# Releasing loads and indirect sends by a count of TensorE instructions, in a local attention and mixture-of-experts kernel

## The chip, the cores and the metric

The kernel runs on 1 core of one Trainium2 chip. The metric is device time in microseconds (us) of one execution, as a median of several runs. Engines are named as in the profile: PE is TensorE's matmul part and PEld its weight loads, DVE is VectorE, ACT ScalarE, POOL GpSimd, SP SyncE. "SPq" and "POOLq" are the sequencers of these engines, which issue DMAs.

## The reference, cut to what matters

Attention comes first: 8 batches, 8 heads, 512 local and 32 global tokens, head size 64. A local query sees the 32 global keys and the local keys within 32 places; a global query sees all. Then each of the 4,608 token rows (512 wide) goes to the one expert of eight that its cosine logit chooses, through two matrices with a ReLU between them.

```python
s_ll = scale * np.matmul(q_l, k_l.transpose(0, 1, 3, 2))
mask = np.abs(pos[:, None] - pos[None, :]) <= window            # window = 32
...
out_l = np.matmul(sm(concat[s_lg, s_ll]), concat[v_g, v_l])
out_g = np.matmul(sm(s_g), v_all)
...
expert_idx = argmax(xn @ en.T / tau)
h = np.maximum(x[mask] @ w1[e], 0.0)
out[mask] = gate_w[mask, None] * (h @ w2[e])
```

## The kernel before, in words

**Two stages.** The first, up to about 238 us, does attention and routing; the second, from about 290 us to the end, runs the experts item by item (`item`, 128 rows at a time, 2 MB of weights for each). Between them lie the last batch's routing, a first block of the expert work in plain f32, and the wait for the table of items.

**Steps of the first stage.** A step `g` is a quarter of a batch (32 steps, and two more to drain). `slot(g)` writes out one step by hand, phase after phase, with automatic reordering off: `scores(g)`, sends, the transposes `turned(g-1)`, `maxima`, `exps`, then `values(g-2)`, and the routing of the batch before (`turn`, `logits`, `back`, `place`, `placed`) with the global tokens' work (`g_scores`, `g_turned`, `g_values`) where `plan` puts it. So three steps are in the air at once, and ACT and DVE have a step's time between the matmuls that feed them and those that need them.

**Instructions of a step.** A f32 matmul is two weight loads and two matmuls on the PE queue, 4 instructions in all; a transpose or a bf16 matmul is 2. One batch (four steps) is scores 448, transposes `turned` 64, `values` 512, `g_values` 192, `g_scores` 64, `g_turned` 24, routing 82: 1,386 instructions, 346 a step.

**Loads.** `loads[g]` lists the DMAs of step `g`, all issued by SP in program order: four of `load_v` (values, tile `vt`, six buffers) and, in most steps, two of `load` (queries and keys, tile `raw`, two buffers); late steps add `fetch_w` (expert weights, tile `stg`), and steps 4 to 7 one `first_fill` each. `deal` takes a step's list at the step's start. `tick(ins, part)` stands at six places of a step (halves of `scores`, end of `turned`, two in `values`, end of `turn`): it sets `state["mark"]` to the PE instruction just written and issues the next sixth of the list. `paced` makes each of these DMAs wait for the mark.

```python
def tick(ins, part):
    state["mark"] = ins
    while parts and share[0] * 6 < part * share[1]:
        parts.pop(0)()
        share[0] += 1
```

**Sends.** When a batch is routed, POOL scatters its rows to their expert's place in HBM with indirect DMAs (`send`, L794, 128 rows each). For batches 0 to 4 these are 20 sends, one a step, in phase SEND behind `scores`, each waiting for the last matmul of that step's scores. POOL also copies the global tokens' rows (L637) and runs a memset for each batch's `choose`.

Of the kernel before, what the change touches and what calls it, by code (L numbers as in the profile page):

```python
# [12 lines left out]
F32 = mybir.dt.float32  # L13
# [17 lines left out]
NE = 8  # L31
# [29 lines left out]
MW = 5 * P  # L61

GCUT = 3


def _window(i):
# [34 lines left out]
def tile_kernel(ctx: ExitStack, tc: tile.TileContext, qk, va, emb, tau, wraw, cst, out):  # L101
# [41 lines left out]
    def give(x, g2, ob):  # L143
# [9 lines left out]
            oob_is_err=False,  # L153
        )

    def early_block(x, h, hT, ob, acc, acc2):


        def turn(src, acc=acc):
            o = acc()  # L160
            for c in range(4):
                nc.tensor.transpose(o[:, c * P : (c + 1) * P], src[:, c * P : (c + 1) * P], ident)
            return o

        st = {}

        def begin(xT, acc):
            st["xT"] = xT
            nc.scalar.copy(xT[:, :512], turn(x, acc))

        def up(nh, ks):
            if ks[0] == 0:
                st["g", nh] = acc()
                if nh == 0:
                    st["h"], st["hT"] = h(), hT()
            for k in ks:
                c = k * 1024 + nh * 512
                nc.tensor.matmul(
                    st["g", nh], st["xT"][:, k * P : (k + 1) * P], cols(st0[0], c, c + 512), start=(k == 0), stop=(k == 3)
                )  # L180
            if ks[-1] == 3:
                nc.scalar.activation(st["h"][:, nh * 512 : (nh + 1) * 512], st["g", nh], AF.Relu)

        def half(nh):
            nc.scalar.copy(st["hT"][:, nh * 512 : (nh + 1) * 512], turn(st["h"][:, nh * 512 : (nh + 1) * 512]))

        def down(ks):
            if ks[0] == 0:
                st["g2"] = acc2()
            for k in ks:  # L190
                nc.tensor.matmul(
                    st["g2"],
                    st["hT"][:, k * P : (k + 1) * P],
                    cols(st0[1], k * 512, (k + 1) * 512),
                    start=(k == 0),
                    stop=(k == 7),
                )
            if ks[-1] == 7:
                give(x, st["g2"], ob())

        return (
            begin,
            lambda: up(0, (0, 1)),
            lambda: up(0, (2, 3)),
            lambda: up(1, (0, 1)),
            lambda: half(0),
            lambda: up(1, (2, 3)),
            lambda: down((0, 1)),
            lambda: half(1),
            lambda: down((2, 3)),  # L210
            lambda: down((4, 5)),
            lambda: down((6, 7)),
        )
# [11 lines left out]
    with ExitStack() as actx:  # L225
# [38 lines left out]
            return after(ins, state["mark"]) if "mark" in state else ins  # L264

        parts = []
        share = [0, 0]

        def tick(ins, part):

            state["mark"] = ins
            while parts and share[0] * 6 < part * share[1]:
                parts.pop(0)()
                share[0] += 1

        def deal(extra):

            while parts:
                parts.pop(0)()
            parts.extend(extra)  # L280
            share[:] = [0, len(parts)]

        def load(b, j, k):

# [67 lines left out]

        def keep_warm(n):
            for _ in range(n):
                nc.tensor.matmul(warm[:, 0], ones[:, :P], ones, start=True, stop=True)  # L355

        zero = pers.tile([P, 1], F32, name="zero")
        nc.gpsimd.memset(zero, 0.0)
# [58 lines left out]
        def setup_turn():  # L417

            em = state["em"]
            ep = bank()  # L420
            for c in range(4):
                nc.tensor.transpose(ep[:, c * NE : (c + 1) * NE], em[:, c * P : (c + 1) * P], ident[:NE, :NE])
            e3 = ep[:, : 4 * NE].rearrange("p (c e) -> p c e", c=4)
            nc.vector.tensor_copy(en[:, :, :NE], e3)

# [15 lines left out]
        def scores(g):  # L441

            b, s = divmod(g, 4)
            raw = state["raw", b]
            state["s", g] = ps = ps_s.tile([P, 2, 512], F32, name="s_ps")
            for k in range(4):
                i = 4 * s + k
                c0 = QW + BQ * _run(_window(i))
                if k // 2 == twin(s):
                    if k % 2 == 0:  # L450
                        for c in range(2):
                            for j in (2 * c, 2 * c + 1):
                                for grp in range(2):
                                    hs = half[grp]
                                    at = 64 * (j % 2)
                                    ins = nc.tensor.matmul(  # L456
                                        ps[at : at + 64, grp, (k + c) * P : (k + c + 1) * P],
                                        raw[hs, j, i * BQ : (i + 2) * BQ],
                                        raw[hs, j, c0 : c0 + P],
                                        start=True,  # L460
                                        stop=True,
                                    )
                else:
                    for j in range(4):
                        for grp in range(2):
                            hs = half[grp]
                            ins = nc.tensor.matmul(  # L467
                                ps[32 * j : 32 * j + 32, grp, k * P : (k + 1) * P],
                                raw[hs, j, i * BQ : (i + 1) * BQ],
                                raw[hs, j, c0 : c0 + P],  # L470
                                start=True,
                                stop=True,
                            )
                if k % 2:
                    tick(ins, 1 + k // 2)
            state["scored"] = ins
            state["nm", g] = sm.tile([P, 8], F32, name="nm")
            state["pb", g] = [sp.tile([P, 512], F32, name="pb") for _ in range(2)]
# [30 lines left out]
        def turned(g, grp):  # L509

            state["tp", g, grp] = pt = bank()
            pb = state["pb", g][grp]
            for k in range(4):
                ins = nc.tensor.transpose(pt[:, k * P : (k + 1) * P], pb[:, k * P : (k + 1) * P], ident)  # L514
            if grp:
                tick(ins, 3)

        def take(g, grp):

# [9 lines left out]
        def values(g):  # L529
# [3 lines left out]
            for grp in range(2):  # L533
                pT = state["pT", g, grp]
                for j in range(4):
                    for k in range(4):
                        ins = nc.tensor.matmul(  # L537
                            po[32 * k : 32 * k + 32, grp, j * VH : (j + 1) * VH],
                            pT[:, col(s, k, j) : col(s, k, j) + 32],
                            vals(b, _window(4 * s + k), grp, j),  # L540
                            start=True,
                            stop=True,
                        )
                tick(ins, 4 + grp)
            state["valued"] = ins

        def normed(g):
# [10 lines left out]
        def g_scores(b, part):  # L558
# [6 lines left out]
            for j in range(4):  # L565
                for grp in range(2):
# [4 lines left out]
                        o = o.rearrange("p (w n) -> p w n", n=96)  # L571
                    else:
                        k = k[:, GCUT * P :]
                    nc.tensor.matmul(o, q, k, start=True, stop=True)  # L574
            gm = state["gm", b]
            for grp in range(2):
                nc.vector.tensor_tensor_reduce(
# [16 lines left out]
        def g_turned(b, part):  # L594
# [2 lines left out]
            state["gt", b, part] = o = bank()  # L597
            if part < 2:
                for c in range(4):
                    nc.tensor.transpose(o[:96, c * P : (c + 1) * P], gp[part][:, c * 96 : (c + 1) * 96], ident)  # L600
            else:
                for c in range(2):
                    for grp in range(2):
                        lo = 416 + 32 * c
                        nc.tensor.transpose(o[:, (2 * c + grp) * P : (2 * c + grp + 1) * P], gp[grp][:, lo : lo + P], ident)

        def g_take(b, part):

# [7 lines left out]
        def g_values(b, grp):  # L616

            og = bank()
            for c, (w, kn) in enumerate(((0, 96), (3, 96), (6, 96), (9, 96), (12, P), (13, P))):
                for j in range(4):  # L620
                    rows = slice(32 * j, 32 * j + 32)
                    nc.tensor.matmul(  # L622
                        og[rows, :VH],
                        gT[:kn, grp, c, rows],
                        vals(b, w, grp, j)[:kn],
# [14 lines left out]
        def route(get, groups, closes=False):  # L640
# [4 lines left out]
            def turn(t):  # L645
# [5 lines left out]
                    st["ss"] = sm.tile([P, NR], F32, name="ss")  # L651
                st["xps", t] = xps = bank()
                for c in range(4):
                    ins = nc.tensor.transpose(xps[:, c * P : (c + 1) * P], x[:, c * P : (c + 1) * P], ident)  # L654

                if t < 4:
                    tick(ins, 6)

            def turn_take(t):

# [13 lines left out]
            def logits(t):  # L674
# [3 lines left out]
                    st["us"] = rt.tile([P, NR * P], F32, name="us", bufs=1)  # L678
                st["u", t] = u = bank()
                for c in range(4):  # L680
                    nc.tensor.matmul(u[32 * c : 32 * c + 32, :n], en[:, c, :], st["xT", t][:, c, :n], start=True, stop=True)  # L681

            def logits_take(t):

# [9 lines left out]
            def back(lo, hi):  # L694
# [2 lines left out]
                    st["lg"] = sm.tile([P, NR, NE], F32, name="lg", bufs=2)  # L697
                st["ut", lo] = ut = bank()
                for t in range(lo, hi):
                    nc.tensor.transpose(ut[:, (t - lo) * P : (t - lo + 1) * P], st["us"][:, t * P : (t + 1) * P], ident)  # L700

            def back_sum(lo, hi):

# [48 lines left out]
            def place():  # L752
# [1 line left out]
                st["pc"] = pc = bank()  # L754

                def add(w, t, lo, hi, start, stop):
                    nc.tensor.matmul(
                        pc[:, lo * NE : hi * NE],
                        w,
                        ohb[:, t : t + hi - lo, :].rearrange("p t e -> p (t e)"),  # L760
# [78 lines left out]
        )  # L839

        plan = {}

        def at(g, phase, f, *args):
            plan.setdefault((g, phase), []).append(lambda: f(*args))
# [28 lines left out]
        for b in range(NB - 1):  # L873
# [17 lines left out]
            for t in range(4):  # L891
# [2 lines left out]
                elif b == NB - 3:  # L894
                    at(g0 + 6 + t // 2, LATE if t % 2 else SEND, r.send, t, "valued" if t % 2 else "scored")
                else:
                    at(g0 + 6 + t, SEND, r.send, t, "scored")

        for b in range(3, NB - 1, 4):
            r, g0 = R["g", b // 4], 4 * b + 7  # L900
# [48 lines left out]
        for g in loads:  # L949
            n = len(loads[g])  # L950
            h = (n + 1) // 2
            loads[g] = [f for pair in zip(loads[g][:h], loads[g][h:] + [None]) for f in pair if f]

        def slot(g):

            def do(phase):
                for f in plan.pop((g, phase), ()):
# [44 lines left out]
        with tc.manual_schedule():  # L1002
            keep_warm(16)
            for g in range(NSTEP + 2):
                slot(g)
            deal([])
            assert not plan, plan


# [382 lines left out]
```

## Time and the profile before

| | us |
|---|---|
| median of 3 runs | 727.18 (725.92 to 728.4) |
| the profiled execution | 725.47 |
| its span in the trace | 723.6 |
| outside the span (725.47 - 723.6) | 1.9 |

The rows below come from the one profiled execution. "issue" as a releaser is time in which an engine waited for nothing that the profile shows. Queue q8 of kind "instruction" carries blocks of the program itself to the engines' sequencers. A row with "xN" stands for N instructions merged.

### The profile page before, as it was taken

Reading aid. Unit: us, or ns where it says so; the run is one execution under the profiler, and the core shown is the slowest. Engines: PE = TensorE matmul, PEld = TensorE weight load, DVE = VectorE, ACT = ScalarE, POOL = GpSimd, SP = SyncE. Lnnn points to the kernel's source line nnn. Section 1 sums busy time; section 2 is a strip of 40 time slices with the busy share of each in tenths; the row PEclk is TensorE's granted clock in tenths of the full one; section 3 lists DMA queues with packets and bytes.
Section 4 is the critical chain, followed back from the end, with each engine's and each line's share of the span. In section 5 each row is a group of like instructions: output and inputs, shape, how many; then the busy total and the mean of one; then the engine's idle time right before and its main releaser. Section 6 shows DMA issues by size and latency. Waiting matters only on the chain.

```text
span 723.6 us, 23361 instructions
## 1 busy us (share of the span) xinstructions
PE 674.1 (93%) x7867; PEld 535.3 (74%) x7869; DVE 422.2 (58%) x1449; ACT 458.6 (63%) x956; POOL 273.0 (38%) x318
## 2 busy tenths in 40 slices
PE   9888878878878998999999999999999999999996
PEld 4666666656756546888888888888888888888885
DVE  2778777888677763545554554545455545455443
ACT  4776767747767365656565666666666656565664
POOL 2011222222212344545454545444454545454543
PEclk9999999999899999999999999999999999999999
DMA  8988989878997257746565665656565746575654
GB/s 274 351 249 258 256 236 279 285 213 292 283 301 227 77 214 267 260 165 249 186 232 205 209 225 193 244 185 248 169 249 179 259 157 240 185 231 206 223 210 156
DMA packets 66588, 165.13 MB, mean 228 GB/s; under 512 B 6548, under 2 KB 14868, under 8 KB 66464
## 3 DMA queue, kind: packets, MB, share of 16 engines
q1 hardware_dynamic: 60704, 145.67, 60.5%
q0 software_dynamic: 5760, 17.87, 7.0%
q8 instruction: 71, 1.16, 0.7%
q14 instruction: 53, 0.43, 0.2%
HBM read 142.49 MB, written 22.07 MB: 227 GB/s over the span
## 4 chain that ended last, share of the span: by engine, by line
PE 88%; issue 5%; DMA 2%; DVE 2%; SPq 1%; ACT 1%; POOL 0%; DVEq 0%; POOLq 0%
PE g L1198 18%; PE g L1199 18%; PE g L1203 18%; PE po L537 5%; PE hps L1221 4%; PE pt L514 4%; PE s_ps L467 4%; PE pt L654 2%; PE xps L1174 2%; PE pt L622 2%; DMA raw<-in_qk_dram 2%; PE po L355 2%; PE pt L574 1%; PE pt L681 1%; PE s_ps L456 1%
## 5 line engine op out<-in xcount | busy, mean ns | idle before, releaser
L1194 DVE TENSOR_TENSOR WL<-stg,WH 128x512 f32 (+1 forms) x144 | 150.5, 1045 | 130.2 <-ACT WH L1192 130.2
L1194 POOL TENSOR_TENSOR WL<-stg,WH 128x512 f32 (+1 forms) x144 | 174.3, 1210 | 88.9 <-ACT WH L1192 87.9
L1192 ACT CAST WH<-stg 128x512 f32 (+1 forms) x288 | 177.4, 618 | 9.2 <-DMA stg<-in_wraw_dram 4.6
L1198 PE MATMUL g<-WH,hH 128*128 (+1 forms) x288 | 119.5, 415 | 0.0
L1198 PE MATMUL g<-WH,xH 128*128 (+1 forms) x288 | 116.0, 403 | 0.0
L1199 PE MATMUL g<-WL,hH 128*128 (+1 forms) x288 | 113.3, 393 | 0.0
L1203 PE MATMUL g<-WH,xL 128*128 (+1 forms) x288 | 112.6, 391 | 0.0
L1199 PE MATMUL g<-WL,xH 128*128 (+1 forms) x288 | 112.5, 390 | 0.0
L147 POOL DMA_INDIRECT out_dram<-ob x37 | 37.2, 1006 | 151.7 <-ACT ob L145 142.4
L507 ACT ACTIVATE pb<-pb,nm 128x128 f32<-128x128 f32 x256 | 80.1, 396 | 11.7 <-DVE nm L490 11.5
L1203 PE MATMUL g<-WH,hL 128*128 (+1 forms) x288 | 83.4, 391 | 0.0
L1224 DVE TENSOR_TENSOR hL<-hps,hH 128x512 fp32r<-128x512 f32 x72 | 49.8, 692 | 53.8 <-ACT hH L1223 53.6
L1203 PEld LDWEIGHTS g<-WH,hL 128*128 128x128 f32 x288 | 54.1, 188 | 12.1
L1203 PEld LDWEIGHTS g<-WH,xL 128*128 128x128 f32 x288 | 54.1, 188 | 11.6
L145 ACT ACTIVATE ob<-g,xr 128x512 f32<-128x512 f32 x36 | 24.8, 688 | 59.5 <-PE g L1203 59.5
L1199 PEld LDWEIGHTS g<-WL,xH 128*128 128x128 f32 x288 | 54.2, 188 | 10.2 <-DVE ob L146 0.2
L1198 PEld LDWEIGHTS g<-WH,xH 128*128 128x128 f32 x288 | 54.2, 188 | 10.2 <-issue 0.2
L1198 PEld LDWEIGHTS g<-WH,hH 128*128 128x128 f32 x288 | 54.4, 189 | 9.5
L1199 PEld LDWEIGHTS g<-WL,hH 128*128 128x128 f32 x288 | 54.4, 189 | 9.1
L1215 ACT ACTIVATE h<-g 128x512 f32<-128x512 f32 x72 | 42.9, 595 | 28.8 <-PE g L1203 28.8
L794 POOL DMA_INDIRECT xs<-xt,si x32 | 32.1, 1004 | 75.9 <-PE pt L514 27.5
L1223 ACT CAST hH<-hps 128x512 fp32r<-128x512 f32 x72 | 42.0, 584 | 24.6 <-PE hps L1221 24.6
(200 smaller groups left out, 985.4 us busy)
## 6 DMA issues: line engine op xcount, KB each, us to landing
stg<-in_wraw_dram SPq DMA_DIRECT2D x36, 2048.0 KB, 9.8
vt<-in_va_dram SPq DMA_DIRECT2D x96, 260.0 KB, 4.7
raw<-in_qk_dram SPq DMA_DIRECT2D x56, 304.0 KB, 5.1
xr<-xs SPq DMA_DIRECT2D x38, 257.0 KB, 2.7
vt<-in_va_dram SPq DMA_DIRECT2D x32, 130.0 KB, 5.1
stg<-in_wraw_dram SPq DMA_DIRECT2D x16, 256.0 KB, 5.5
xs<-fill SPq DMA_DIRECT2D x12, 257.0 KB, 3.0
stg<-in_wraw_dram SPq DMA_DIRECT2D x4, 512.0 KB, 7.1
```

What stands on the lines that cost most here:

```text
L147: nc.gpsimd.indirect_dma_start(out=out[:, :], out_offset=bass.IndirectOffsetOnAxis(ap=ob[:, DM : DM + 1].bitcast(U32), axis=0), in_=ob[:, ...
L507: nc.scalar.activation(pb[:, cs], pb[:, cs], AF.Exp, bias=nm[:, n : n + 1], scale=-1.0)
L537: ins = nc.tensor.matmul(po[32 * k : 32 * k + 32, grp, j * VH : (j + 1) * VH], pT[:, col(s, k, j) : col(s, k, j) + 32], vals(b, _window(4 ...
L794: ins = nc.gpsimd.indirect_dma_start(out=xs[:, :], out_offset=bass.IndirectOffsetOnAxis(ap=st["si"][:, t : t + 1], axis=0), in_=get(t), in ...
L1192: made.append(nc.scalar.copy(WH[:, ds(ra, 1), cs], s3))
L1194: made.append(eng.tensor_tensor(WL[:, ds(r, 1), cs], s3, WH[:, ds(r, 1), cs], ALU.subtract))
L1198: reads.append(nc.tensor.matmul(o.unsqueeze(1), a, WH2[:, ds(rp, 1), sl], start=first, stop=False))
L1199: reads.append(nc.tensor.matmul(o.unsqueeze(1), a, WL2[:, ds(rp, 1), sl], start=False, stop=False))
L1203: reads.append(nc.tensor.matmul(o.unsqueeze(1), a, WH2[:, ds(rp, 1), sl], start=False, stop=last))
L1215: nc.scalar.activation(h[:, nh * 512 : (nh + 1) * 512], g, AF.Relu)
L1223: nc.scalar.copy(hv, hp_)
L1224: nc.vector.tensor_tensor(hL[:, nh * 4 : nh * 4 + 4, :].rearrange("p c n -> p (c n)"), hp_, hv, ALU.subtract)
```

## The change

`tick` loses its six fixed places. Every matmul and transpose of the first stage now goes through `matmul` or `transpose`, which count PE instructions in `begun` (4 or 2 each; `slot` adds `WAITS` = 3 a step for waits on the PE queue) and call `tick`. When `begun` plus 62 reaches instruction 2, 5, 8, 11 or 14 of a block of 256, the matmul just written becomes the mark and one DMA is taken from the list. `deal` no longer empties the list at a step's start: it leaves up to 2 DMAs of the step before, and issues the others at once, behind the last mark. The 20 sends of batches 0 to 4 leave phase SEND and become the third entry of their step's list, waiting for the same kind of mark. The later batches' sends and the second stage are as before.

```diff
+FETCH = 256
+FIRST = 62
+MARKS = (2, 5, 8, 11, 14)
+SPARE = 2
+WAITS = 3
...
+    def counted(ins, n):
+        begun[0] += n
+        for f in seen:
+            f(ins)
+        return ins
+    def matmul(out, lhsT, rhs, start, stop):
+        return counted(nc.tensor.matmul(out, lhsT, rhs, start=start, stop=stop), 4 if lhsT.dtype == F32 else 2)
+    def transpose(out, in_, eye):
+        return counted(nc.tensor.transpose(out, in_, eye), 2)
...
-        def tick(ins, part):
-            state["mark"] = ins
-            while parts and share[0] * 6 < part * share[1]:
-                parts.pop(0)()
-                share[0] += 1
+        def tick(ins):
+            n, k = divmod(ahead[0], len(MARKS))
+            while begun[0] + FIRST >= n * FETCH + MARKS[k]:
+                state["mark"] = ins
+                if parts:
+                    parts.pop(0)()
+                ahead[0] += 1
+                n, k = divmod(ahead[0], len(MARKS))
         def deal(extra):
-            while parts:
+            while len(parts) > SPARE or (parts and not extra):
                 parts.pop(0)()
             parts.extend(extra)
-            share[:] = [0, len(parts)]
...
-                    at(g0 + 6 + t, SEND, r.send, t, "scored")
+                    sends[g0 + 6 + t] = r.send, t, "mark"
...
+            if g in sends:
+                loads[g].insert(2, lambda a=sends[g]: a[0](*a[1:]))
+        seen.append(tick)
         def slot(g):
+            begun[0] += WAITS
```

## Rows read from the trace of the kernel before

**Rows 1.** Busy time by stretch: us, each engine's busy us (instructions), PEclk, DMA share, GB/s.
```profile
12.00:40.00 28.00, 24.77 (x669) 18.91 (x673) 19.16 (x127) 18.77 (x50) 0.00 (x0) 0.94 0.94 306
...
40.00:236.00 196.00, 160.18 (x4802) 127.69 (x4794) 152.35 (x914) 135.00 (x366) 41.88 (x97) 0.97 0.85 263
236.00:290.00 54.00, 51.05 (x268) 30.65 (x257) 31.59 (x112) 26.89 (x45) 23.41 (x21) 1.00 0.54 190
290.00:723.00 433.00, 427.75 (x2085) 353.74 (x2083) 216.88 (x280) 274.07 (x487) 203.03 (x174) 1.00 0.61 211
```

**Rows 2.** The chain that ended last, 40 to 236 us: shares, then pieces (start, us, what).
```profile
by line: PE po L537 17.6%; issue 16.0%; PE pt L514 13.6%; PE s_ps L467 10.5%; PE pt L654 7.6%; PE pt L622 6.0%; PE pt L574 4.5%; PE s_ps L456 3.9%; PE pt L681 3.8%; PE pt L600 3.0%; PE pt L700 1.6%; PE pt L605 1.6%; DVE xt L555 1.4%; ACT pb
...
52.98 1.16 issue
...
177.05 2.40 issue
...
231.25 1.16 issue
```

**Rows 3.** DMA queues, 40 to 236 us: packets, MB, share of 16 engines.
```profile
q1 hardware_dynamic: 24768, 44.22, 75.2%
q0 software_dynamic: 2000, 6.58, 8.5%
q8 instruction: 38, 0.62, 1.3%
```

**Rows 4.** Busy time by stretch, cut where PE resumes after a block's edge.
```profile
173.65:179.45 5.80, 3.40 (x126) 2.76 (x127) 5.30 (x34) 4.00 (x12) 1.29 (x4) 1.00 0.88 306
179.45:183.86 4.41, 4.41 (x126) 3.88 (x130) 2.31 (x20) 2.16 (x6) 0.99 (x1) 0.65 0.49 86
183.86:189.60 5.74, 3.51 (x139) 2.54 (x131) 3.06 (x12) 3.56 (x9) 1.14 (x4) 0.98 1.00 353
```

**Rows 5.** Timeline of PE: start, us, instruction, count, idle time before it.
```profile
173.65 0.82 PE L537 MATMUL po<-vt,pT 128*32 128x65 f32 x41 [0.24 <-issue]
...
179.45 1.07 PE L467 MATMUL s_ps<-raw 64*32 64x128 f32 x53 [2.40 <-issue]
```

**Rows 6.** DMA queues, 177.2 to 177.3 us.
```profile
q1 hardware_dynamic: 21, 0.03, 70.4%
q8 instruction: 1, 0.02, 60.5%
```

**Rows 7.** DMA queues, 180.5 to 180.6 us.
```profile
q8 instruction: 1, 0.02, 83.3%
```

**Rows 8.** DMA queues, 187.2 to 187.3 us.
```profile
q8 instruction: 1, 0.02, 61.9%
```

**Rows 9.** Timeline of SP's DMA issues: start, us, line, what, count.
```profile
172.65 0.38 SPq L300 DMA_DIRECT2D vt<-in_va_dram  x1
173.12 0.38 SPq L288 DMA_DIRECT2D raw<-in_qk_dram  x1
...
175.83 4.62 SPq L300 DMA_DIRECT2D vt<-in_va_dram  x2
...
182.82 0.41 SPq L288 DMA_DIRECT2D raw<-in_qk_dram  x1
183.33 0.43 SPq L300 DMA_DIRECT2D vt<-in_va_dram  x1
```

**Rows 10.** DMA issues of the whole run: count, KB each, median us to landing.
```profile
vt<-in_va_dram SPq DMA_DIRECT2D x96, 260.0 KB, 4.7
raw<-in_qk_dram SPq DMA_DIRECT2D x56, 304.0 KB, 5.1
...
xs<-xt,si POOLq DMA_INDIRECT x32, 5.9
```

**Rows 11.** Busy time by stretch, two of the half-clock ones.
```profile
74.92:78.33 3.41, 3.41 (x72) 3.19 (x73) 2.35 (x14) 3.41 (x11) 1.00 (x1) 0.50 0.78 221
...
190.97:194.38 3.41, 3.41 (x72) 3.19 (x72) 2.31 (x14) 3.41 (x11) 0.89 (x1) 0.50 0.85 239
```

More of the change, by code (lines that the diff above doesn't have):

```diff
@@ L154, in give @@
         )
+    begun = [0]
+    seen = []
+    def counted(ins, n):
[7 more added lines that the diff above has]
+        return counted(nc.tensor.transpose(out, in_, eye), 2)
     def early_block(x, h, hT, ob, acc, acc2):
@@ L161, in turn @@
             for c in range(4):
-                nc.tensor.transpose(o[:, c * P : (c + 1) * P], src[:, c * P : (c + 1) * P], ident)
+                transpose(o[:, c * P : (c + 1) * P], src[:, c * P : (c + 1) * P], ident)
             return o
@@ L177, in up @@
                 c = k * 1024 + nh * 512
-                nc.tensor.matmul(
+                matmul(
                     st["g", nh], st["xT"][:, k * P : (k + 1) * P], cols(st0[0], c, c + 512), start=(k == 0), stop=(k == 3)
@@ L190, in down @@
             for k in ks:
-                nc.tensor.matmul(
+                matmul(
                     st["g2"],
@@ L266, in tile_kernel @@
         parts = []
-        share = [0, 0]
-        def tick(ins, part):
-            state["mark"] = ins
-            while parts and share[0] * 6 < part * share[1]:
-                parts.pop(0)()
-                share[0] += 1
+        ahead = [0]
+        def tick(ins):
[6 more added lines that the diff above has]
+                n, k = divmod(ahead[0], len(MARKS))
         def deal(extra):
-            while parts:
+            while len(parts) > SPARE or (parts and not extra):
                 parts.pop(0)()
             parts.extend(extra)
-            share[:] = [0, len(parts)]
         def load(b, j, k):
@@ L354, in keep_warm @@
             for _ in range(n):
-                nc.tensor.matmul(warm[:, 0], ones[:, :P], ones, start=True, stop=True)
+                matmul(warm[:, 0], ones[:, :P], ones, start=True, stop=True)
         zero = pers.tile([P, 1], F32, name="zero")
@@ L421, in setup_turn @@
             for c in range(4):
-                nc.tensor.transpose(ep[:, c * NE : (c + 1) * NE], em[:, c * P : (c + 1) * P], ident[:NE, :NE])
+                transpose(ep[:, c * NE : (c + 1) * NE], em[:, c * P : (c + 1) * P], ident[:NE, :NE])
             e3 = ep[:, : 4 * NE].rearrange("p (c e) -> p c e", c=4)
@@ L455, in scores @@
                                     at = 64 * (j % 2)
-                                    ins = nc.tensor.matmul(
+                                    ins = matmul(
                                         ps[at : at + 64, grp, (k + c) * P : (k + c + 1) * P],
@@ L466, in scores @@
                             hs = half[grp]
-                            ins = nc.tensor.matmul(
+                            ins = matmul(
                                 ps[32 * j : 32 * j + 32, grp, k * P : (k + 1) * P],
@@ L473, in scores @@
                             )
-                if k % 2:
-                    tick(ins, 1 + k // 2)
             state["scored"] = ins
@@ L513, in turned @@
             for k in range(4):
-                ins = nc.tensor.transpose(pt[:, k * P : (k + 1) * P], pb[:, k * P : (k + 1) * P], ident)
-            if grp:
-                tick(ins, 3)
+                ins = transpose(pt[:, k * P : (k + 1) * P], pb[:, k * P : (k + 1) * P], ident)
         def take(g, grp):
@@ L536, in values @@
                     for k in range(4):
-                        ins = nc.tensor.matmul(
+                        ins = matmul(
                             po[32 * k : 32 * k + 32, grp, j * VH : (j + 1) * VH],
@@ L543, in values @@
                         )
-                tick(ins, 4 + grp)
             state["valued"] = ins
@@ L573, in g_scores @@
                         k = k[:, GCUT * P :]
-                    nc.tensor.matmul(o, q, k, start=True, stop=True)
+                    matmul(o, q, k, start=True, stop=True)
             gm = state["gm", b]
@@ L599, in g_turned @@
                 for c in range(4):
-                    nc.tensor.transpose(o[:96, c * P : (c + 1) * P], gp[part][:, c * 96 : (c + 1) * 96], ident)
+                    transpose(o[:96, c * P : (c + 1) * P], gp[part][:, c * 96 : (c + 1) * 96], ident)
             else:
@@ L604, in g_turned @@
                         lo = 416 + 32 * c
-                        nc.tensor.transpose(o[:, (2 * c + grp) * P : (2 * c + grp + 1) * P], gp[grp][:, lo : lo + P], ident)
+                        transpose(o[:, (2 * c + grp) * P : (2 * c + grp + 1) * P], gp[grp][:, lo : lo + P], ident)
         def g_take(b, part):
@@ L621, in g_values @@
                     rows = slice(32 * j, 32 * j + 32)
-                    nc.tensor.matmul(
+                    matmul(
                         og[rows, :VH],
@@ L653, in turn @@
                 for c in range(4):
-                    ins = nc.tensor.transpose(xps[:, c * P : (c + 1) * P], x[:, c * P : (c + 1) * P], ident)
-                if t < 4:
-                    tick(ins, 6)
+                    ins = transpose(xps[:, c * P : (c + 1) * P], x[:, c * P : (c + 1) * P], ident)
             def turn_take(t):
@@ L680, in logits @@
                 for c in range(4):
-                    nc.tensor.matmul(u[32 * c : 32 * c + 32, :n], en[:, c, :], st["xT", t][:, c, :n], start=True, stop=True)
+                    matmul(u[32 * c : 32 * c + 32, :n], en[:, c, :], st["xT", t][:, c, :n], start=True, stop=True)
             def logits_take(t):
@@ L699, in back @@
                 for t in range(lo, hi):
-                    nc.tensor.transpose(ut[:, (t - lo) * P : (t - lo + 1) * P], st["us"][:, t * P : (t + 1) * P], ident)
+                    transpose(ut[:, (t - lo) * P : (t - lo + 1) * P], st["us"][:, t * P : (t + 1) * P], ident)
             def back_sum(lo, hi):
@@ L756, in add @@
                 def add(w, t, lo, hi, start, stop):
-                    nc.tensor.matmul(
+                    matmul(
                         pc[:, lo * NE : hi * NE],
@@ L841, in tile_kernel @@
         plan = {}
+        sends = {}
         def at(g, phase, f, *args):
@@ L1006, in tile_kernel @@
             deal([])
+            seen.clear()
             assert not plan, plan
```

## The prediction, put on record before the run

> **What bounds the kernel now.** I cut the span into stages first [rows 1]. From 290 us on PE is busy 427.75 of 433 us, and the change leaves that stage alone: it only starts earlier or later. Between 40 and 236 us PE is busy 160.2 of 196 us, so there is something to win there, and nowhere else that the change touches.
>
> The chain of waits of that stretch says what fills the gap [rows 2]: 16.0% of 196 us, 31.4 us, is "issue", waiting for nothing that the profile shows. Of its pieces 14 are over 1.1 us (the first at 52.98, the last at 231.25; together 24.2 us). The other 7.2 us are small.
>
> What the waits are: between two resumes of PE the busy table counts 253 and 256 weight loads and matmuls, then 270 with those that lie across the cuts [rows 4]. So PE stops at the edge of a block of 256. Queue q8 moved 38 packets in the same stretch, 0.62 MB, 16 KB each [rows 3]: one block of program for each edge. Three neighbouring blocks show when. PE resumes at 173.65; the fetch starts between 177.2 and 177.3 [rows 6], 3.6 us later; PE has waited 2.40 us when it goes on at 179.45 [rows 5], 2.2 us after the fetch began. From 179.45 the next fetch starts after 1.1 us [rows 7] and there is no wait at 183.86. From 183.86 the next starts after 3.4 us [rows 8], and PE goes on 2.3 us behind it, at 189.60.
>
> What sets 1.1 against 3.5 us is what SP had issued just before the edge [rows 9]: two loads in the last 1.0 us before 173.65, two before 183.86, but none in the 3.6 us before 179.45 (the second of the two that the row at 175.83 holds ends it, a us behind the edge). After 179.45 the DMA engines moved 86 GB/s, around the other two 306 and 353 [rows 4]. The fetch stands behind the loads. As a PE that waits releases no loads, late and free fetches tend to take turns.
>
> **The marks.** The change releases loads just after an edge, five together. Does it hit the edge? I counted the timeline's PE instructions from the first one on and set the source's count beside them: the edges fall where `begun` + 62 is 2 (first steps) to 18 (last) short of a multiple of 256, because the queue holds a few more waits than 3 a step. So mark 2 comes 4 to 20 instructions behind the edge and mark 14 16 to 32 behind it. At 253 instructions in some 3.4 us of work [rows 4] that is 0.05 to 0.45 us. On the right side throughout.
>
> **The pace.** A batch holds 1,386 counted instructions and 12 for waits, 5.46 blocks, 27.3 marks; its list has 16 `vt`, 8 `raw` and 4 sends, 28. They balance; a load or so a step is left to `deal` and goes out at a step's start, anywhere in a block. I count that as nothing for the end, but it keeps some fetches hindered.
>
> **The sum.** (a) A fetch with nothing ahead brings the block 1.1 + 2.3 = 3.4 us after an edge. A block's own work is (196 - 31.4) / 38 = 4.3 us on average, so most edges would not wait; short blocks still would. The 24 edges without a long wait lose 7.2 / 24 = 0.3 us each. If all 38 did: 38 x 0.3 = 11.4 left of 31.4, 20.0 won. That is the upper bound. The lower is 0: 0.83 us an edge as now.
>
> (b) Which end? The five transfers of a block are 28 of these 260 and 304 KB [rows 10] in 5.46 blocks, about 1.4 MB. The stretch moves 263 GB/s at a share of 0.85 [rows 1], 309 when full: 4.5 us. If the first data come about as late as a free fetch, 1.1 us, the queue is empty 5.6 us after the edge, and the next fetch is free if the block lasted 5.6 - 1.1 = 4.5 us. The mean is 4.3 without waits. So long blocks are followed by a free fetch and runs of short ones by one 1 us late: much nearer to free than the 3.5 us of now. I take 0.4 us an edge, 15.2 left, 16.2 won.
>
> (c) Two rules of the Trainium skill bear on this. "Runtime: NRT & Kernel Launch", section Instruction fetch mechanics, has instructions come in blocks of 16 KiB, 256 instructions, prefetched, the crossing "mostly hidden"; the size agrees with 16 KB a packet, the hiding does not: 2.40 us at one edge. By the rule (a) and (b) would be 0 and the time 727.
>
> (d) Half clock. In three stretches of 3.41 us (74.92, 180.73 and 190.97) PE had a granted clock of 0.50, the lower of its two levels, 1.2 GHz [rows 11]; each begins within 1.5 us of PE resuming from a wait of over 2 us. In them it did 72 matmuls; at the stretch's mean, 4802 in 160.2 us, it does 102. Lost: 1.0 us each, 3.0 in all. Bounds 0 and 3; I take 1.5, since the waits shrink but do not all go.
>
> (e) Given back. The work of 196 us is to fit into some 178. DVE is busy 152.4, 78% now and 86% then; the DMA share goes from 0.85 to 0.93, about what it was at 306 GB/s from 12 to 40 us. Some waits on DVE, ACT and loads that now end while PE stands at an edge will show. Bounds: 0, and half of (b), 8; nearer to 0, as a step's work lies a step ahead of its use. I take 3.
>
> (f) The start. In step 0 two of batch 1's loads now stand ahead of the fourth part of the first loads; with the change step 0's four wait for step 1. Two loads are 608 KB, 2.0 us at 306 GB/s. Batch 1 is wanted later, the first part sooner; the DMAs are full either way. 2.0 us of gain or loss, taken as 0.
>
> (g) The sends. Twenty leave their place behind a step's scores for a mark, some us sooner or later. Behind one on POOL stand the copies of L637 and a memset; POOL is busy 41.9 of 196 us and the rows are read only by the second stage, so nothing is taken. Without that slack it would be a send's 5.9 us to landing, once. On SP behind each waiting load stand the next loads and fills, all wanted a step or more later. Counting is done when the program is written, and a mark is a signal of an instruction that is there anyway: 0.
>
> Sum: 16.2 + 1.5 - 3 = 14.7 us; 725.47 (723.6 of span, 1.9 around it) - 14.7 = 710.8. The median of the runs is 1.7 above this execution: 712.5.
>
> **Rivals.** Nearly all won (0.10): 20.0 + 3.0, nothing given back: 704 less up to 2 at the start, 702 to 705. For it: the free edges of now lose 0.3 on average. Against: the DMA share would be 0.85 x 196 / 173 = 0.96.
>
> Half lost again (0.14): PE, freed from the fetch, waits for loads and DVE. A residual of 0.6 us an edge wins 31.4 - 22.8 = 8.6; with 1.5 from (d) and 3 to 8 given back, 2 to 7 are left: 720 to 725. For it: DMA share 1.00 in the block that ends at 189.60 [rows 4]. Against: no load is seen to hold PE long in this stretch.
>
> No change (0.09): the loads are not what delays the fetch, or the five have never drained by the next edge, so that 0.83 an edge stays: 725 to 729. For it: 5.6 us against blocks of 4.3. By "DMA: Bandwidth & Descriptors", section Queues, rings and completion order, each DMA engine takes the queues in turn, a packet at a time; by that, a load could hold a fetch up by one packet only and this rival would hold. The 3.6 and 3.4 us against it.
>
> Slower (0.09): the marks slip to before the edge. It needs the changed program to hold about 4 fewer waits on the PE queue early, or 20 fewer late, than now. Then five loads stand ahead of each fetch, and each edge waits like one of the 14, between 2.40 and 1.16 us [rows 2]: 38 x 1.8 = 68, 37 more than now: 764. If only the first third slips, 739.
>
> **How the numbers follow.** My forecast, 705 to 719, has 0.58. With nearly-all-won and half-lost that is 0.82 faster. Within 0.3% (2.2 us, about what these runs can tell) 0.09, slower 0.09. From 702 to 725 lies the forecast, most of the first rival and nearly all of the second: 0.8.
>
> **What would show it.** In the changed profile, between 40 us and the end of this stage: "issue" down from 16% to about 8%; few pieces over 1.1 us; q8 packets that start 1.1 to 1.7 us behind an edge, not 3.5; SP's issues in groups of five right behind the edges; fewer half-clock stretches; the DMA share over 0.9; and the second stage beginning some 15 us sooner with its 433 us as they were. I am wrong if fetches still start late (then not the loads before the edge, or not drained), if SP's groups stand ahead of edges (the count), or if "issue" falls and waits on DVE, ACT or loads rise as much.

## The result, and the profile after

The changed kernel is slower: 732.56 us against 728.84 us, medians of 22 runs each on the same chip; the ratio is 1.0058, with a 95% interval of 1.0036 to 1.0079. The forecast was 712.5 us. Chips differ by as much as the change does (the kernel before had medians of 721.4 to 728.8), so every ratio below is against runs of the kernel before on the same chip. The ratios leave out executions over 1.5% above the fastest of their kernel (1,093.95 us in e7 and 1,960.1 us in e10 among them), and e1's profile is of one of these, 731.53 us against a median of 723.84 us of the others. The profiled execution took 734.59 us with a span of 732.7, 9.1 longer than that of before.

Busy time by stretch of the changed kernel: us, each engine's busy us (instructions), PEclk, DMA share, GB/s.

```profile
40.00:236.00 196.00, 157.72 (x4613) 124.86 (x4603) 146.56 (x893) 131.19 (x358) 39.51 (x89) 0.95 0.84 260
...
299.00:732.00 433.00, 427.75 (x2085) 353.57 (x2083) 216.52 (x280) 274.17 (x487) 202.73 (x174) 1.00 0.61 211
```

The second stage is what it was [rows 1], 9 us later. In the same 196 us PE does 4,613 matmuls of the first stage instead of 4,802. The chain of waits says why, with its shares and five longest pieces, 40 to 236 us:

```profile
by line: PE pt L177 24.2%; PE s_ps L174 14.4%; PE pt L174 13.0%; PE po L174 12.9%; issue 11.3%; DMA raw<-in_qk_dram 8.9%; DMA vt<-in_va_dram 6.6%; ACT pb L530 1.2%; DVE pb L513 0.8%; DVE xt L575 0.7%; DVE junk L688 0.6%; DVE gp L597 0.4%; S
...
57.99 6.87 DMA vt<-in_va_dram
82.34 5.32 DMA raw<-in_qk_dram
120.02 4.02 DMA vt<-in_va_dram
140.31 6.07 DMA raw<-in_qk_dram
172.74 6.03 DMA raw<-in_qk_dram
```

"issue" went from 16.0% [rows 2] to 11.3%, 31.4 to 22.1 us. But the loads, which were not among the shown shares of the chain before, now hold 15.5% of it. A piece runs from a load's issue to its landing; what PE itself lost is in the table of its waits (instruction, releaser: us, times, longest), 40 to 236 us:

```profile
PE po L174 <- issue: 9.1, 6, 2.6
PE pt L174 <- DMA vt<-in_va_dram: 8.0, 3, 4.1
PE pt L174 <- issue: 6.4, 5, 2.3
PE s_ps L174 <- DMA raw<-in_qk_dram: 6.2, 3, 3.7
PE s_ps L174 <- issue: 4.1, 6, 1.1
PE pt L177 <- issue: 0.2, 1, 0.2
```

That is 19.8 us of "issue" and 14.2 us of loads. The same table of the kernel before has 30.0 us of "issue" and no load:

```profile
PE s_ps L467 <- issue: 10.6, 6, 2.4
PE po L537 <- issue: 9.7, 11, 2.0
PE pt L622 <- issue: 6.1, 5, 1.9
PE pt L574 <- issue: 3.4, 2, 1.7
...
PE pt L681 <- issue: 0.2, 1, 0.2
```

In these two profiles 10.2 us were won at the edges and 14.2 lost on loads.

One of the six waits in full. SP issues the last load of batch 6's `raw`, the 48th of that tile, in the second row; in the third PE begins that batch's scores, and in the last it goes on when the load is there (timelines of the changed kernel: start, us, what, count, idle time before).

```profile
172.32 0.33 SPq L325 DMA_DIRECT2D vt<-in_va_dram  x1
172.74 0.38 SPq L313 DMA_DIRECT2D raw<-in_qk_dram  x1
```
```profile
174.53 0.65 PE L174 MATMUL s_ps<-raw 64*64 64x128 f32 x12
178.91 1.04 PE L174 MATMUL s_ps<-raw 64*64 64x128 f32 x36 [3.72 <-DMA raw<-in_qk_dram]
```

The load goes out 1.8 us before the scores of its batch begin and takes 6.0 us. The same pair in the kernel before: issued 6.7 us ahead, no wait.

```profile
163.98 0.33 SPq L288 DMA_DIRECT2D raw<-in_qk_dram  x1
```
```profile
170.64 0.67 PE L456 MATMUL s_ps<-raw 64*64 64x128 f32 x16
```

Behind this wait PE is at half clock for a while. The busy table of two stretches of the changed kernel, the wait and what follows:

```profile
174.50:178.90 4.40, 0.68 (x13) 0.44 (x13) 2.64 (x13) 2.11 (x7) 0.00 (x0) 1.00 0.95 299
180.20:183.60 3.40, 3.40 (x87) 3.07 (x88) 1.83 (x16) 2.56 (x8) 0.46 (x1) 0.50 0.03 10
```

### The profile page after: what moved, and what is told of

Read it like the earlier page. It is cut to its first block, busy times and chain, and to the rows that moved or that the text cites. A ratio compares the mean times of both kernels' runs of the same rounds, so it can differ in the third digit from the quotient of the medians.

```text
span 732.7 us, 23337 instructions
## 1 busy us (share of the span) xinstructions
PE 679.0 (93%) x7867; PEld 538.4 (73%) x7869; DVE 420.7 (57%) x1449; ACT 458.4 (63%) x956; POOL 271.7 (37%) x318
## 4 chain that ended last, share of the span: by engine, by line
PE 85%; DMA 6%; issue 4%; DVE 2%; ACT 1%; SPq 1%; POOL 0%; DVEq 0%; POOLq 0%; ACTq 0%
PE g L1224 18%; PE g L1225 18%; PE g L1229 18%; PE pt L177 8%; PE po L174 7%; PE pt L174 5%; PE s_ps L174 5%; PE hps L1247 4%; DMA raw<-in_qk_dram 3%; PE xps L1200 2%; DMA vt<-in_va_dram 2%; DMA stg<-in_wraw_dram 1%; PE g L174 1%; ACT pb L530 1%; SPq L1095 0%
## 5 line engine op out<-in xcount | busy, mean ns | idle before, releaser
L174 PE MATMUL s_ps<-raw 64*32 64x128 f32 (+1 forms) x1792 | 49.9, 291 | 13.6 <-DMA raw<-in_qk_dram 7.1
```

Of the source, the lines that this page charges most:

```text
L174: return counted(nc.tensor.matmul(out, lhsT, rhs, start=start, stop=stop), 4 if lhsT.dtype == F32 else 2)
```

## The experiments

All of them are the changed kernel with the edit shown. Theory L says that loads are issued late, B that five released together land late, A that the place of the release against the edge counts, N that it does not. Where a row below is a run's, "issue" and "loads" are sums over its table of PE's waits from 40 to 236 us, as above, unless the text says otherwise; the granted clock is of the same stretch.

| run | ratio (95% interval) | issue, us | loads, us | PEclk |
|---|---|---|---|---|
| before | 1 | 30.0 | 0 | 0.97 |
| changed | 1.0058 (1.0036 to 1.0079) | 19.8 | 14.2 | 0.95 |
| e1 seven marks | 1.0018 (0.9993 to 1.0043) | 27.2 | 3.1 | 0.90 |
| e2 raw a step earlier | 1.0071 (1.0050 to 1.0092) | 19.2 | 8.7 | 0.93 |
| e3 even marks | 0.9972 (0.9943 to 1.0001) | 22.1 | 0.4 | 0.98 |
| e4 sends back | 1.0072 (1.0046 to 1.0098) | 20.3 | 7.1 | 0.92 |
| e5 mid block | 1.0155 (1.0114 to 1.0195) | 27.5 | 4.0 | 0.94 |
| e6 six even marks | 1.0024 (0.9989 to 1.0058) | 22.7 | 0 | 0.98 |
| e7 seven, raw earlier | 1.0192 (1.0148 to 1.0236) | 27.0 | 3.7 | 0.92 |
| e8 changed again | 1.0107 (1.0066 to 1.0147) | 23.2 | 7.3 | 0.97 |
| e9 even again | 1.0017 (0.9990 to 1.0044) | 24.9 | 1.1 | 0.97 |
| e10 front marks | 1.0004 (0.9975 to 1.0033) | 19.9 | 0 | 0.98 |
| e11 even, sends back | 0.9964 (0.9936 to 0.9993) | 19.1 | 0.3 | 0.97 |
| e12 front, sends back | 0.9960 (0.9929 to 0.9992) | 23.8 | 0.3 | 0.99 |

The waits are those of one profiled execution each, the ratios those of 3 to 21; single executions of one kernel lie up to 2% apart, but for the two named above. The changed kernel was profiled twice (changed and e8), and its two profiles differ by 3.4 us of "issue" and 6.9 us of loads: differences of that size between two rows of the table show nothing by themselves.

**e1, seven marks.** More places behind each edge.

```diff
-MARKS = (2, 5, 8, 11, 14)
+MARKS = (2, 5, 8, 11, 14, 17, 20)
```


> MARKS gets two more places, 17 and 20, so that up to seven DMAs go out behind each edge and no step's list (six to nine DMAs) is carried past the next edge. Theory L (loads are issued late: 27.3 marks a batch for 28 DMAs, two left over at each step, so a step's last load goes out almost a step later than before): PE's own waits on loads from 40 us to the end of the first stage, 14.2 us in the changed kernel, fall under 4 us; the waits named issue stay near 20 us; the run is 8 to 15 us faster than the changed kernel, ratio to the kernel before 0.985 to 0.995. Theory B (five transfers released together land late, whenever they are released): with seven together the waits on loads stay at 14 us or grow, ratio 1.005 to 1.02.

PE's waits in e1:

```profile
PE po L174 <- issue: 9.6, 6, 2.6
PE pt L174 <- issue: 8.8, 8, 3.0
PE s_ps L174 <- issue: 8.8, 4, 3.5
PE pt L174 <- DMA vt<-in_va_dram: 3.1, 3, 2.0
```

The loads' waits are 3.1 us, as L said and against B, "issue" is 27.2 us and the granted clock 0.90. But this profile is of an execution of 731.53 us, while the ratio is that of eight with a median of 723.84 us, so these figures don't explain it. By the ratio the time gains 0.4% on the changed kernel, not 1 to 2%: L's forecast of the time missed.

**e2, raw a step earlier.**

```diff
-                    later(max(4 * b - 5 + j, 0), load, b, j, k)
+                    later(max(4 * b - 6 + j, 0), load, b, j, k)
```


> The loads of raw are listed one step earlier, all else as in the changed kernel. Both theories say that lead is what is short: PE's waits on raw (6.2 us) fall under 1 us, those on vt (8.0 us) stay within 6 to 11 us; with less half clock the run is 5 to 9 us faster than the changed kernel, ratio to the kernel before 0.993 to 1.000. If neither holds and raw is late because DMA as a whole is short, the wait moves to vt and the ratio stays 1.004 to 1.008.

The waits on `raw` are gone and 8.7 us on `vt` stay, as expected: it is lead that `raw` was short of. The ratio, 1.0071, misses the 0.993 to 1.000 that both theories gave and is not better than that of the changed kernel, with the clock at 0.93. So lead alone, given to one of the two, buys no time.

**e3, even marks.** As many places, spread over the block.

```diff
+MARKS = (2, 53, 104, 155, 206)
```


> MARKS become 2, 53, 104, 155, 206: as many places, spread over the block, the same list and carrying over. Theory L: waits on loads stay at 8 us or more, as issue is as late; issue grows back towards 31 us; ratio to the kernel before 1.01 to 1.02. Theory B: waits on loads fall under 4 us as nothing is bunched, issue grows to 31 us, ratio 0.997 to 1.003.

PE's waits and the timeline of SP and PE around batch 6's last `raw` load in e3:

```profile
PE pt L174 <- issue: 10.0, 10, 2.3
PE po L174 <- issue: 6.6, 5, 2.0
PE s_ps L174 <- issue: 5.5, 5, 1.4
PE s_ps L174 <- DMA raw<-in_qk_dram: 0.4, 1, 0.4
```
```profile
161.36 0.76 SPq L313 DMA_DIRECT2D raw<-in_qk_dram  x1
```
```profile
166.54 1.27 PE L174 MATMUL s_ps<-raw 64*64 64x128 f32 x48
```

Both theories missed a half. The waits on loads vanish, so L is wrong in saying that the number of places made the loads late: the number is the same here. The 48th load goes out 5.2 us ahead instead of 1.8. What made it late is the lump: with all five places behind an edge, a load that is next in line waits for the whole next block, wherever the step ends. And "issue" does not come back to 31 us but stays at 22.1, without any care for the edges.

**e4, sends back.**

```diff
-                    sends[g0 + 6 + t] = r.send, t, "mark"
+                    at(g0 + 6 + t, SEND, r.send, t, "scored")
```


> The 20 sends go back to their place behind a step's scores, the loads stay on the marks: a batch's list is then 24 DMAs for 27.3 marks. Theory L: fewer are carried over, waits on loads fall from 14.2 to between 3 and 9 us, and the run is 3 to 8 us faster than the changed kernel, ratio to the kernel before 0.994 to 1.002. Theory B: waits on loads stay 12 to 16 us, ratio 1.003 to 1.010.

The waits on loads are 7.1 us (5.2 on `vt`, 1.9 on `raw`), in L's range; but the changed kernel itself has 7.3 us in its second profile (e8), so that the sends take places from loads is not shown. The ratio is B's, with the clock at 0.92.

**e5, mid block.** The same five marks, half a block behind the edge.

```diff
-FIRST = 62
+FIRST = 190
```


> FIRST becomes 190, so the same five marks stand half a block behind the edge, about 2 us later. Theory A (the place counts: a burst right behind an edge has mostly drained by the next one): now a burst reaches over the next edge and its fetch stands behind it; PE's idle time at edges, 21 us in the changed kernel, rises over 33 us; ratio to the kernel before 1.015 to 1.04. Theory N (the place does not count: five loads are 4.5 us of transfer in blocks of 4.3 us, so a fetch meets loads wherever they are released): idle at edges 18 to 26 us, ratio 1.003 to 1.012.

"issue" is 27.5 us, against 19.8 and 23.2 in the two profiles of the changed kernel; A asked for over 33, N for under 26. The ratio, 1.0155, is A's, clear of the changed kernel's first ratio but not of the interval of its second (e8, up to 1.0147). So the place seems to count for a lump, by some 4 to 8 us of "issue" between single profiles; this is not firm.

**e6, six even marks.**

```diff
+MARKS = (2, 44, 87, 130, 172, 215)
```


> Six marks spread over the block (2, 44, 87, 130, 172, 215): spread as in the run with five even ones, but 32.8 places a batch for 28 DMAs, so almost nothing is carried over. Theory R (an even release is what helps; carrying over costs little when nothing is bunched): waits on loads under 1 us, idle at edges 20 to 25 us, ratio to the kernel before 0.992 to 1.000, as with five. If the fifth of places more makes the loads crowd, the idle time at edges goes to 27 us or more and the ratio to 1.000 to 1.006.

No wait on loads and 22.7 us of "issue", as expected; the ratio, 1.0024, is above the 0.992 to 1.000 of theory R and can't be told from 1.

**e7, seven marks and raw a step earlier**, the edits of e1 and e2 together.

> Seven marks behind the edge and raw listed a step earlier: the two cures for late loads together, the release still bunched at edges. Theory L alone (late loads are all that is wrong with the change): waits on loads under 1.5 us, idle at edges 20 us, ratio to the kernel before 0.982 to 0.992. With theory N beside it (bunching at the edge wins nothing at edges and sets PE to half clock more often): waits on loads under 1.5 us too, but idle at edges 24 to 30 us and half clock over 25 us, ratio 0.997 to 1.006.

It has the highest ratio of all, above what either theory allowed, and its waits on loads (3.7 us) missed the 1.5 us of both; "issue", 27.0 us, is in N's range. Its profile is much like that of e1, but the two profiled executions are only 0.6% apart (735.6 and 731.53 us). That its ratio is 1.7% above that of e1 is not explained by them and stays open.

**e8, the changed kernel again**, with no edit, on another chip.

> The changed kernel itself, beside the others on one chip. Theory L+B (what it loses are waits on loads, from issue that comes later and in lumps): ratio to the kernel before 1.003 to 1.012, PE's waits on loads 9 to 18 us, idle at edges 18 to 25 us. If the loss was the first chip's, the ratio is 0.998 to 1.002.

Slower again, by more: 1.0107. The chain of waits of this profile has pieces like those of the first, 40 to 236 us; four of its five longest are on loads:

```profile
by line: PE pt L177 22.3%; PE po L174 14.2%; PE s_ps L174 14.0%; issue 12.9%; PE pt L174 12.8%; DMA raw<-in_qk_dram 7.2%; DMA vt<-in_va_dram 4.5%; ACT pb L530 1.8%; DVE xt L575 1.1%; DVE junk L688 0.9%; DVE pb L513 0.8%; ACT pT L542 0.6%; D
...
57.25 5.88 DMA vt<-in_va_dram
80.06 5.01 DMA raw<-in_qk_dram
...
137.46 5.21 DMA raw<-in_qk_dram
170.53 3.83 DMA raw<-in_qk_dram
```

PE's waits on loads in e8:

```profile
PE pt L174 <- DMA vt<-in_va_dram: 4.8, 2, 3.7
PE s_ps L174 <- DMA raw<-in_qk_dram: 2.5, 3, 1.7
```

They are 7.3 us, half of the first profile's and below the 9 expected. The profiled execution, 724.86 us, is the fastest of e8's four. The 48th `raw` load goes out 1.6 us ahead here (170.53 and 172.14 us), against 1.8.

**e9, even marks again**, the edit of e3, five rounds.

> The five even marks once more, with five rounds. Theory L+B: an even release keeps the loads in time (waits on them under 2 us) and idle at edges at 19 to 25 us; ratio to the kernel before 0.990 to 0.999, and under that of the changed kernel by at least 0.006. If the earlier 0.997 was chance, 0.999 to 1.006.

1.0017: e3's 0.9972 was in part chance. It is 0.9% under the changed kernel on the same chip (e8), with intervals apart, and no faster than the kernel before. PE's only wait on loads in e9:

```profile
PE pt L174 <- DMA vt<-in_va_dram: 1.1, 1, 1.1
```

**e10, front marks.**

```diff
+MARKS = (2, 34, 66, 98, 130)
```


> Marks at 2, 34, 66, 98, 130: even, but in the first half of the block, so that the last load goes out half a block ahead of the next edge. If the place of the edge counts beside evenness (theory A with L), idle at edges falls to 12 to 20 us and waits on loads stay under 4 us: ratio 0.985 to 0.996. If the place does not count (theory N), idle at edges stays 19 to 25 us and the ratio is that of the even marks, within 0.004.

"issue" is 19.9 us, 5 below e9 and in the ranges of both theories, and loads are in time; the ratio is that of the even marks within 0.004, as N had it. If the place saves "issue", the time does not show it.

**e11, even marks with the sends back**, the edits of e3 and e4.

> Five even marks, and the 20 sends back behind their step's scores: 24 DMAs on 27.3 marks a batch. Theory: sends cost nothing either way, waits on loads under 2 us, idle at edges 19 to 26 us, ratio within 0.004 of the even marks alone. If sends at arbitrary places hold up fetches, idle at edges rises over 27 us and the ratio by over 0.004.

0.9964 with an interval clear of 1, and 0.5% under e9 on the same chip: the sends do better behind the scores than in the line, which was not expected. By what, the runs do not show.

**e12, front marks with the sends back**, the edits of e10 and e4.

> Marks at 2, 34, 66, 98, 130 and the sends back behind their step's scores: both things that lowered the idle time at edges without waits on loads. If they add up: idle at edges 13 to 18 us, waits on loads under 2 us, ratio to the kernel before 0.988 to 0.996. If each only moves the same waits about: idle at edges 17 to 22 us, ratio 0.996 to 1.001.

0.9960: as good as e11 and no better. The ratio lies where the two expected ranges meet, and "issue", 23.8 us, is above both. Busy time of e12, 40 to 236 us:

```profile
40.00:236.00 196.00, 164.92 (x4840) 126.23 (x4829) 157.92 (x949) 136.51 (x368) 45.86 (x102) 0.99 0.85 270
```

These two beat the kernel before by 0.4%, with intervals that just clear 1. e11 also beats the changed kernel, by 1.4% on the same chip (0.9964 against the 1.0107 of e8); e12 had no run of the changed kernel beside it.

## Why the prediction was wrong, by its own steps

**What bounds the kernel** held as far as these profiles tell: the waits named "issue" fell when the release changed, and fetches still start late where loads were issued just before an edge (below). e5 points the same way, less firmly. "DMA: Bandwidth & Descriptors" of the Trainium skill, section Queues, rings and completion order, has each DMA engine change queues after each packet; no run here shows how many packets a fetch stood behind.

**The marks** were right: behind the edges at 99.60 and 213.21 us, where PE goes on after a wait named "issue", SP's next issues are at 99.97 and 213.67, some 0.4 us later.

**(a) and (b), the edges.** 10.2 us were won where 16.2 were forecast, and 6.8 in e8. 19.8 us over the 36 q8 packets of the changed profile's stretch is 0.55 us an edge, not 0.4. At 16 edges of that stretch PE went on after a wait named "issue" of 0.3 us or more. At ten of them SP had issued a load in the last 3 us before PE went on, and the next q8 packet began 2.4 to 4.6 us after that; at the other six it began 1.1 to 2.0 us after. So the fetch mostly began as early as (a) said where no load had just gone out, but the marks did not keep loads away from the next edge. The fifth load behind the edge at 222.46 us went out at 225.22, 2.6 us before PE went on at the next edge, 227.78; and `deal` issues others at a step's start. And what the alignment was to win, an even release wins too, without looking at edges (e3 22.1, e6 22.7, e9 24.9 us).

**(d), the clock,** had the wrong sign in the first profile: from 40 to 236 us PE was at a granted clock of 0.50 for 20.5 us, against 13.6 before. In e8's profile it was 10.2 us. The prediction's reading of the kernel before left out a fourth stretch, from 153.42 us; PE did 108 matmuls in it, more than the 102 of the mean, so the lost 1.0 us does not hold for each stretch. Over whole runs, the four of e8 have a mean granted clock of 0.983, the kernel before on the same chip 0.987; at (1 - clock) x 2 of the run that is 25 us at half clock against 19. Over the 22 runs of the changed kernel the time rises by 0.31 us for each us at half clock, so these 6 us go with some 2 us. The clock goes with the lump: the groups of runs with five or seven marks in a lump have mean clocks of 0.974 to 0.983, those with marks spread over the block or its first half 0.985 to 0.989, the kernel before 0.983 to 0.988.

**(e), given back, is the step that failed.** It stood at 3 us, "nearer to 0, as a step's work lies a step ahead of its use". 14.2 us were lost on loads in the first profile, and 7.3 in e8, where that is more than the 6.8 us won at the edges. Two of the tiles are wanted sooner than I took it: the last `raw` of a batch is listed two steps before its scores and had 6.7 us in hand, not a step more than its landing; the last `vt` of a batch is wanted by `g_values` in the very next step, and all three waits on `vt` in the first profile are there (PE goes on at 65.00, 124.18 and 184.91 us). **The pace** counted what is left over by `deal` as nothing. The runs showed that it matters, though not through the number of places (e3, e9): a lump of five with two left over puts the last of a list behind the next edge, and the 48th `raw` load went from 6.7 to 1.8 us of lead (5.2 with even marks, e3). I had the rival, "half lost again", at 0.14, and bounded (e) by half of (b), 8 us, with no row on the lead of the last load; the bound was no bound.

**The sends, (g),** were taken as 0. In the line they cost about 0.5% with even marks (e9 against e11); that they do so by taking places from loads is not shown (e4). **(f), the start,** stayed within its 2.0 us: the first scores of batch 1 went on after their wait for `raw` at 30.46 us, against 29.49 before.

In all, in the first profile: -10.2 us at the edges up to 236 us (-8.5 to the end of the stage, where one more wait, of 1.7 us, ends at 240.09), +14.2 on loads, and some +4 by the clock (35.8 us at half clock in the whole profiled run against 22.7, at 0.31): 8 to 10 us, and the span grew by 9.1. These are single profiles; the medians differ by 3.7 us on the first chip and 7 on the second. In e8's profile the same account comes to nothing: 30.5 us of "issue" and loads together against 30.0, and less half clock, in an execution 3.5 us above its chip's median of the kernel before. So that the lump costs the time is shown, by e9 against e8 on one chip, and that it makes the last loads late, by their leads; how the lost time divides between late loads and the clock is open. It is also open what shorter waits at edges are worth: e9 has 5 us less of them than the kernel before in the profiles and no better time.

## What to carry to other kernels

Before moving a load's release, list for each tile the last load's issue and its first use, and take the least of these leads, not the usual one: the tightest pays. A release that wins one queue's wait by bunching takes lead from the loads at the end of the bunch; spreading by a count of instructions won about as much at the edges here and kept enough lead (5.2 us of 6.7, against 1.8 with the lump). A wait moved from often and short to seldom and long may cost more than its length: here PE was at half clock for 3.4 us behind one of 3.7 us. Profile the same kernel twice before reading a difference between two profiles: here the waits on loads were 14.2 us once and 7.3 us the other time.

## What the runs showed of the hardware that was not expected

At the edges of the kernel before shown above, PE went on 2.2 to 2.3 us after the packet of a 16 KB block of program had started, and PE stood for one up to 2.6 us in the changed kernel too. The time of single executions goes with the share at half clock: from 0.23 to 0.60 us for each us, in the groups of 10 runs and more of this study, with correlations of 0.45 to 0.90; that the clock causes all of it is not shown.
